# Forward and gradients of two attention and two gated MLP layers: more transposes made by DMA, weight loads moved, a saved tensor laid out by pairs of tiles

## The chip, the cores and the metric

The kernel runs on one core of one Trainium2 chip, as one launch. The metric is the device time in microseconds, given as the median of the runs shown. A profiled execution is one run of its own; the trace and the profile come from it. The engines are TensorE (PE: matmuls and transposes; PEld: its weight loads), VectorE (DVE), ScalarE (ACT), GpSimd (POOL) and SyncE (SP). SP issues all the DMAs of this kernel; a "queue of SP" is the order in which it does so, and an issue that has to wait for a semaphore holds up all issues behind it. A DMA with `transpose=True` transposes blocks on its way.

## The reference

Everything is bf16; S = 2048 rows, D = 512, F = 1376, 32 heads of 16. The input passes through four residual layers, A, B, A, B, and both A layers use the same weights, as do both B layers:

```
def _A_ref(x, wqkv, wo):                 # linear attention, phi(t) = t+1 if t > 0 else exp(t)
    q, k, v = heads of (x @ wqkv)
    pq, pk = phi(q), phi(k)
    kv = einsum("bhsd,bhse->bhde", pk, v);  z = sum of pk over s
    o = (pq . kv) / (pq . z + 1e-6)
    return o @ wo
def _B_ref(x, w_gate, w_up, w_down):
    return (sigmoid(x @ w_gate) * (x @ w_up)) @ w_down
x = A_x
x = x + _A_ref(_layernorm(x), A_wqkv, A_wo);  x = x + _B_ref(_layernorm(x), B_w_gate, B_w_up, B_w_down)
x = x + _A_ref(_layernorm(x), A_wqkv, A_wo);  x = x + _B_ref(_layernorm(x), B_w_gate, B_w_up, B_w_down)
```

The outputs are x and, for a given gradient of it, the gradients of A_x, A_wqkv, A_wo, B_w_gate, B_w_up and B_w_down (a gradient of a weight is the sum over its two layers).

## The kernel before

**Tiles and stages.** The rows are cut into 16 tiles of 128 (`st` 0 to 15); x stays in SBUF in f32. The four layers have the numbers 0 to 3. The program runs through these stages, with the times of the profiled execution: `kq_fwd` of layer 0 (keys and queries, 0 to 64 us); `ab_fwd`, which ends the attention of layer 0 and computes the MLP of layer 1 ("layer 1" below, 64 to 216 us); `kq_fwd` of layer 2 (to 290 us); `ab_fwd` for layers 2 and 3 ("layer 3", to 408 us); then backward `b_bwd_p1` of layer 3 (to 545 us), `a_bwd_p1` of layer 2 (phase 1 to 610 us, a short chain of products, phase 2 to 685 us), a stretch of weight gradients alone (to 747 us), `b_bwd_p1` of layer 1 (to 885 us), `a_bwd_p1` of layer 0 (phase 1 to 953 us, phase 2 to 1030 us), and the rest of the weight gradients (the "tail", to the end).

**Order of the work.** The order on TensorE, VectorE, ScalarE and GpSimd is the order in which the program is written (`manual_schedule`). The order of SP's queue is made by a scheduler from the order of the program and from what each DMA depends on; `issue_after(x)` pins a DMA behind the instruction x.

**`ab_fwd`, one tile.** The products g and u (L906) in three slices of 512, 512 and 352 columns; ScalarE's sigmoids (L908); VectorE's hh = u * sigmoid(g) (L911); GpSimd's second factor (L912); the attention output of a later tile (L868); then hh is transposed and multiplied by w_down one tile later (`finish`, L935). hh is transposed in one of two ways: on TensorE, in 4+4+3 blocks, with ScalarE copying them out of PSUM (L920, L923), or by one DMA (`dma_T`, L928), for which GpSimd first clears the padding of the tile. `HH_DMA` (L816) says which tiles go by DMA: 10 to 14 in layer 1, 2 to 14 in layer 3. In tiles that go by DMA, the copies of the transposed layer norm (hT) go to ScalarE instead of VectorE. At the end of a tile its saved tensors are stored (`ssd`, `hdd` and `hdl`; the last is the last piece of hh), and `side[st]` is called: in layer 1 it runs one of 13 **weight units** of `wT_units`, each of which loads up to 512 columns of a weight transposed by DMA (`wt_st`), its store to DRAM following with the next unit (wdT, wuT, wgT, woT and wqkvT: the backward pass reads them from there); in layer 3 it is a load of a backward weight, at tiles 2, 5 and 8.

**Backward attention, `a_bwd_p1`.** At its start `load_a_weights` (L251) loads woT, wqkvT and MT. Phase 1, per tile: the product dp (L1549) of MT and the transposed gradient of the tile; a chain on VectorE that ends in dq, which overwrites `phq_ld`; every second tile `dqk_store` (L1464) stores the dq of two tiles. The gradient is transposed on TensorE for tiles 0 to 7 (`gT`), and for tiles 8 to 11 and 12 to 15 by one DMA each from `g_all` (`gTb`, L1504), issued at tiles 4 and 8 (`GTLOAD`). Then GT (L1577). Phase 2, per tile: `T2_ps` (L1702), the transposes of dq and, for tiles 0 to 3, of pk, on TensorE, with ScalarE's copy to `pdT`; the product dpk (L1707); VectorE's dk, transposed on TensorE (L372); and `finish` (L1674), 12 matmuls of the transposed dq, pk and dk with weights. Inputs are loaded by pairs of tiles: `pk_ld`, `dq_ld` (two loads), `hT_ld`, `h_ld` (L1100, L1608) and, from tile 4 on, `pkT` transposed by DMA (L1599) behind hT.

**Weight gradients, `P2`.** These are products over all 16 tiles, cut into jobs of up to 256 columns. A job reads a set of saved columns (`p2_set`, L1298; three buffers, loaded up to two jobs ahead) and multiplies it with h (`p_a`; L1440) or with the gradient (L1424). ScalarE copies the result of layers 3 and 2 to an output stage `dw_stg`, which is stored to DRAM (L1397); for layers 1 and 0 VectorE adds that part to the result (L1414) and the sum goes to the output. The stage has two buffers. `W.run(n)` runs n pieces of jobs; phase 1 slips one behind each tile. In the tail they run without other work, and between them `a_small_grads` (L1760) loads saved matrices transposed and computes the rest of the gradients of A, with outputs in `fin_o`, a tile that comes from the same pool as the stage.

**The saved dq and dk.** `sv_dqk` (L111) has the dimensions [group of 256 columns, partition, tile, column]: `dqk_store` writes 512 bytes per row and group, and a set load reads 8 KB per partition in one run.

Of the kernel before, what the change touches and what calls it, by code (L numbers as in the profile page):

```python
# [18 lines left out]
D = 512  # L19
# [41 lines left out]
def kernel(  # L61
# [42 lines left out]
    for l in range(4):  # L104
        d = {}
        d["h"] = dram.tile([S, D], BF16, name=f"sv_h{l}")
        d["gbf"] = dram.tile([S, D], BF16, name=f"sv_gbf{l}")
        if l % 2 == 0:
            for nm in ("hT", "pqn", "phq", "pk"):
                d[nm] = dram.tile([S, D], BF16, name=f"sv_{nm}{l}")  # L110
            d["dqk"] = dram.tile([2 * D // GW, P, NST, GW], BF16, name=f"sv_dqk{l}")  # L111
            d["X"] = dram.tile([D, D], BF16, name=f"sv_X{l}")
            d["G"] = dram.tile([D, D], BF16, name=f"sv_G{l}")
            for nm, w in SMALL:
                d[nm] = dram.tile([P, NDC, w], BF16, name=f"sv_{nm}{l}")
            d["MT"] = dram.tile([D, D], BF16, name=f"sv_MT{l}")
        else:
            d["ssd"] = dram.tile([S, 2, F], BF16, name=f"sv_ssd{l}")
            d["hdd"] = dram.tile([3, NG, P, NST, GW], BF16, name=f"sv_hdd{l}")
            d["hdl"] = dram.tile([3, P, NST, F - NG * GW], BF16, name=f"sv_hdl{l}")  # L120
        k.sv[l] = d
    k.wT = dict(
        wqkvT=dram.tile([3 * D, D], BF16, name="wqkvT_d"),
        woT=dram.tile([D, D], BF16, name="woT_d"),
# [16 lines left out]
    with tc.tile_pool(name="wfwd", bufs=1, reuse_waits="tile") as wfwd, ExitStack() as lctx, tc.manual_schedule(engines=EM):  # L141
# [44 lines left out]
        with tc.tile_pool(name="aq0", bufs=1, reuse_waits="tile") as aq:  # L186
            A = kq_fwd(k, aq, 0, lns[0], lns[1], x_bf)
            with tc.tile_pool(name="wt_stage", bufs=2, reuse_waits="tile") as wt_stage:
                units = wT_units(k, wt_stage, A_wqkv, A_wo, B_w_gate, B_w_up, B_w_down)
                A.tail()  # L190
                ab_fwd(k, A, lns[1], {st + 1: u for st, u in enumerate(units)}, nxt=lns[2])
# [54 lines left out]
    if True:  # L246
        def load_b_weights():
            for ld in b_weight_loads():
                ld()

        def load_a_weights(l):  # L251
            woT_GT = wb.tile([P, 2, NDC, D], BF16, name="woT_GT", tag="w_b")
            k.woT, k.GT = woT_GT[:, 0, :, :], woT_GT[:, 1, :, :]
            nc.sync.dma_start(out=k.woT, in_=k.wT["woT"].rearrange("(c p) j -> p c j", p=P))
            k.wqkvT = wb.tile([P, 3 * NDC, D], BF16, name="wqkvT", tag="w_a")
            nc.sync.dma_start(out=k.wqkvT[:], in_=k.wT["wqkvT"].rearrange("(c p) j -> p c j", p=P))
# [66 lines left out]
        with tc.manual_schedule(engines=EM):  # L323
# [3 lines left out]
            sg = a_small_grads(k, tail, R.stage)  # L327
# [66 lines left out]
def wT_units(k, stage, A_wqkv, A_wo, B_w_gate, B_w_up, B_w_down):  # L394
# [33 lines left out]
    for src, nm, C in ((A_wo, "woT", D), (A_wqkv, "wqkvT", 3 * D)):  # L428
        for c0 in range(0, C // P, NDC):
            units.append(by_rows(src, c0, NDC, k.wT[nm]))  # L430

    def step():
        old = stores[:]
        stores.clear()
        if units:
            units.pop(0)()
        for store in old:
            store()
    return [step] * (len(units) + 1)
# [376 lines left out]
HH_DMA = {1: range(10, NST - 1), 3: range(2, NST - 1)}  # L816
# [70 lines left out]
def ab_fwd(k, A, ln, side, nxt=None, out_cb=None, last_cb=None):  # L887
# [3 lines left out]
    with ExitStack() as ctx:  # L891
# [61 lines left out]
        for st in range(NST):  # L953
# [3 lines left out]
                     hh=wide.tile([P, FP], BF16, name="hh_t"),  # L957
# [66 lines left out]
            nc.sync.dma_start(out=sv["hdl"][0, :, st, :], in_=T["hh"][:, NG * GW:F])  # L1024
            if st in side:
                side[st]()
# [269 lines left out]
def p2_set(k, R, src):  # L1296
    t = R.sets.tile([P, NST, R.set_w], BF16, name="p2_set")
    R.eng().dma_start(out=t[:, :, 0:src.shape[-1]], in_=src)  # L1298
# [25 lines left out]
def a_jobs(k, l):  # L1324
    return [("wqkv", k.sv[l]["dqk"][g, :, :, :], g * GW, GW) for g in range(2 * D // GW)]
# [7 lines left out]
class P2:  # L1333
# [67 lines left out]
    def units(self):  # L1401
        k, R, nc = self.k, self.R, self.k.nc
        i = 0
        while True:
# [5 lines left out]
            ov = p2_stage_tile(R, "b")  # L1410
# [50 lines left out]
def dqk_store(k, sv, half, b, nb, src):  # L1461
    n = D // GW
    for g in range(n):
        k.nc.sync.dma_start(out=sv["dqk"][half * n + g, :, b * nb:(b + 1) * nb, :],  # L1464
                            in_=src[:, :, g * GW:(g + 1) * GW])


def a_bwd_p1(k, R, l, W, mk_out_cb=None):
# [6 lines left out]
    with ExitStack() as ctx:  # L1475
# [9 lines left out]
        with tc.tile_pool(name=f"ab_stg1{l}", bufs=3, side="right", reuse_waits="tile") as stg, \  # L1485
# [38 lines left out]
            def dq_ops(T):  # L1524
# [9 lines left out]
                if st % NB2 == NB2 - 1:  # L1534
                    dqk_store(k, sv, 0, st // NB2, NB2, T["ph_pair"][:])
# [7 lines left out]
            for st in range(NST):  # L1543
                ph_st = phld.get(st)
                T = dict(st=st, ph=ph_st, ph_pair=phld.cur)
# [40 lines left out]
        with tc.tile_pool(name=f"ab_stg2{l}", bufs=2, side="right", reuse_waits="tile") as stg, \  # L1586
# [14 lines left out]
            def load(p):  # L1601
# [5 lines left out]
                for g in range(D // GW):  # L1607
                    nc.sync.dma_start(out=dq[:, :, g * GW:(g + 1) * GW], in_=sv["dqk"][g, :, st0:st0 + NB2, :])  # L1608
                hTld.get(st0)
                LD[p] = dict(pk=pkld.cur, dq=dq, hT=hTld.cur)  # L1610
                if st0 >= NB:
                    with tc.issue_after(hTld.ins.ins):
                        load_pkT(p)
# [76 lines left out]
            for st in range(NST):  # L1690
                L = LD[st // NB2]
                e = st % NB2
                pk_st, dq_st, hT_st = L["pk"][:, e, :], L["dq"][:, e, :], L["hT"][:, e, :]
# [4 lines left out]
                pdT = work.tile([P, 2, NDC, P], BF16, name="pdT")  # L1698
                tps = ps_tile(k, "t", [P, 2, NDC, P], BF16, "T2_ps")
                for a, src in enumerate((dq_st, pk_st)[0:1 + own]):  # L1700
                    for c in range(NDC):
                        nc.tensor.transpose(tps[:, a, c, :], src[:, c * P:(c + 1) * P], k.ident[:])  # L1702
                nc.scalar.copy(pdT[:, 0:1 + own, :, :], tps[:, 0:1 + own, :, :])
                T["dqT"] = pdT[:, 0, :, :]
                T["pkT"] = pdT[:, 1, :, :] if own else pkT[st // NB2][:, :, e * P:(e + 1) * P]
# [7 lines left out]
                if e == NB2 - 1:  # L1713
                    dqk_store(k, sv, 1, st // NB2, NB2, dkst[:])
# [45 lines left out]
def a_small_grads(k, pool, stg):  # L1760
# [13 lines left out]
    for c in range(NDC):  # L1774
# [3 lines left out]
        o = stg.tile([P, D], BF16, name="fin_o")  # L1778
# [3 lines left out]
    for ic in range(NDC):  # L1782
# [5 lines left out]
        o = stg.tile([P, D], BF16, name="fin_o")  # L1788
# [33 lines left out]
```

## Time and profile before

| what | value |
| --- | --- |
| runs before | 1160.11, 1161.38, 1163.07 us; median 1161.38 us |
| profiled execution | 1164.9 us, of which the span of the trace is 1163.2 us |
| TensorE clock, mean granted | 0.999 of full speed |
| busy, share of the span | PE 97%, DVE 60%, ACT 46%, POOL 25% |
| DMA | 281.33 MB in 365220 packets, 242 GB/s on average |
| SP's data queue | 82.0% of 16 DMA engines' span |

The span is the time between the first and the last instruction of the trace; the device time has 1.7 us around it. A busy share is the time in which an engine has at least one instruction under way. The DMA share is the time that packets took, as a part of what 16 DMA engines have; the trace has it above 1 in some short windows. In lines of the timeline, the first number is the start and the second the duration in microseconds, followed by engine, source line, operation, output and inputs, shape and count; a bracket tells how long the engine was idle before, and what released it. A line of windows gives the window, its length, the busy time and number of instructions of PE, PEld, DVE, ACT and POOL, then the granted clock, the DMA share and GB/s.

### The profile page before, as it was taken

The numbers are of one execution on the slowest core, as the hardware profiler recorded it, in microseconds if no ns is written. First come the engines' busy times: TensorE is split into PE (matmuls) and PEld (weight loads), VectorE is DVE, ScalarE is ACT, GpSimd is POOL, SyncE is SP. The second block draws the span as 40 slices with busy tenths as digits, with TensorE's granted clock in tenths as the row PEclk, the third lists the DMA queues.
The fourth block names the chain that finished last, engine by engine and source line by source line (L and its number), as shares of the span: only waits on it lengthen the run. The fifth ranks groups of instructions, "written<-read, shape, count | busy, mean of one in ns | idle before, by whom it ended". The sixth has DMA issues, their size and how long they took to land.

```text
span 1163.2 us, 20084 instructions
## 1 busy us (share of the span) xinstructions
PE 1127.2 (97%) x7414; PEld 672.2 (58%) x7524; DVE 698.3 (60%) x1343; ACT 529.8 (46%) x983; POOL 287.7 (25%) x514
## 2 busy tenths in 40 slices
PE   8979999998999999999999999999999999999988
PEld 4445444444455555555456578855557755548878
DVE  6778876667767456664975740166664976741211
ACT  6667666546665644444625531244344516510001
POOL 5646667435666400000110120000000111210000
PEclk9999999999999999999999999999999999999999
DMA  8969997858677899997889979468977788859985
GB/s 267 304 185 267 286 267 218 253 157 282 202 209 229 252 273 284 312 278 223 221 243 273 283 207 344 119 191 245 275 248 235 192 280 246 224 185 298 262 185 167
DMA packets 365220, 281.33 MB, mean 242 GB/s; under 512 B 141184, under 2 KB 350016, under 8 KB 360256
## 3 DMA queue, kind: packets, MB, share of 16 engines
q1 hardware_dynamic: 365120, 280.03, 82.0%
q8 instruction: 59, 0.97, 0.3%
q14 instruction: 41, 0.34, 0.1%
HBM read 136.71 MB, written 117.80 MB: 219 GB/s over the span
## 4 chain that ended last, share of the span: by engine, by line
PE 87%; DVE 6%; DMA 4%; ACT 2%; issue 1%; POOL 0%; DVEq 0%; ACTq 0%; SPq 0%; POOLq 0%
PE p_ps L1440 17%; PE dh_ps L1200 13%; PE dh_ps L1674 7%; PE p_ps L1424 7%; PE dhh_ps L1077 6%; PE u_ps L906 5%; PE g_ps L906 5%; PE y_ps L935 5%; PE T_ps L1160 3%; PE GT_ps L1577 2%; PE dp_ps L1549 2%; PE dpk_ps L1707 2%; PE y_ps L868 2%; PE t_mm L613 2%; PE X_ps L621 2%
## 5 line engine op out<-in xcount | busy, mean ns | idle before, releaser
L1440 PE MATMUL p_ps<-p_set,p_a 128*128 128x256 bf16 (+1 forms) x2032 | 211.4, 265 | 3.4 <-DVE dw_stg L1414 3.3
L1440 PEld LDWEIGHTS <-p_a 128*128 128x128 bf16 x2048 | 186.2, 98 | 26.7 <-DMA p_set<-sv_dqk 2.3
L1085 DVE TENSOR_TENSOR dd<-dhh_ps,ssd 128x512 bf16<-128x512 f32 x144 | 82.5, 629 | 129.9 <-PE dhh_ps L1077 128.9
L1164 ACT COPY ddT<-T_ps 128x1024 bf16<-128x1024 bf16 (+1 forms) x96 | 83.0, 867 | 132.1 <-PE T_ps L1160 131.7
L912 POOL TENSOR_TENSOR ssd_t<-hh_t,oms 128x512 bf16<-128x512 bf16 (+1 forms) x96 | 101.5, 1064 | 47.7 <-ACT hT L381 24.7
L1200 PEld LDWEIGHTS <-ddT 128*128 128x128 bf16 (+1 forms) x704 | 68.7, 98 | 72.2
L1051 POOL TENSOR_SCALAR ab<-c 128x2 f32<-128x2 f32 x64 | 12.3, 192 | 393.1 <-DVE junk L1048 378.9
L906 PEld LDWEIGHTS <-hT 128*128 128x128 bf16 x768 | 72.2, 98 | 63.8 <-DVE hT L379 1.4
L911 DVE TENSOR_TENSOR hh_t<-u_ps,ssd_t 128x512 bf16<-128x512 f32 (+1 forms) x96 | 60.5, 634 | 61.7 <-PE u_ps L906 42.8
L1414 DVE TENSOR_TENSOR dw_stg<-p_ps,dw_stg 128x512 bf16<-128x512 f32 (+3 forms) x43 | 28.0, 654 | 109.0 <-PE p_ps L1440 82.5
L906 PE MATMUL u_ps<-wu,hT 128*128 128x512 bf16 (+1 forms) x379 | 89.6, 357 | 0.5
L906 PE MATMUL g_ps<-wg,hT 128*128 128x512 bf16 (+1 forms) x366 | 86.5, 356 | 1.7 <-DVE hT L379 1.0
L1200 PE MATMUL dh_ps<-wgT,ddT 128*128 128x512 bf16 (+1 forms) x344 | 84.8, 379 | 0.3
L908 ACT ACTIVATE ssd_t<-g_ps 128x512 bf16<-128x512 f32 (+1 forms) x96 | 53.3, 555 | 66.4 <-PE g_ps L906 58.3
L935 PE MATMUL y_ps<-wd,hhT 128*128 128x512 bf16 (+1 forms) x346 | 80.5, 379 | 0.9 <-DVE x L937 0.6
L1200 PE MATMUL dh_ps<-wuT,ddT 128*128 128x512 bf16 (+1 forms) x340 | 80.7, 379 | 0.6
L1424 PE MATMUL p_ps<-p_a,p_set 128*128 128x512 bf16 (+1 forms) x344 | 80.4, 379 | 0.4
L1043 ACT ACTIVATE t_sb<-dh_ps,rstd_all 128x512 f32<-128x512 f32 x64 | 44.0, 687 | 77.5 <-issue 41.8
L1077 PE MATMUL dhh_ps<-wdT,gTb 128*128 128x512 bf16 (+1 forms) x328 | 73.3, 357 | 0.4
L1048 DVE SCALAR_TENSOR_TENSOR junk<-t_sb,h_ld 128x512 bf16<-128x512 f32 x64 | 44.0, 688 | 42.9 <-ACT t_sb L1043 42.1
L935 PEld LDWEIGHTS <-hhT 128*128 128x128 bf16 (+1 forms) x352 | 33.9, 98 | 39.3 <-issue 0.7
L1424 PEld LDWEIGHTS <-p_set 128*128 128x128 bf16 (+1 forms) x352 | 33.5, 100 | 34.9
(225 smaller groups left out, 1914.5 us busy)
## 6 DMA issues: line engine op xcount, KB each, us to landing
p_set<-sv_hdd SPq DMA_DIRECT2D x30, 1024.0 KB, 7.3
sv_ssd<-ssd_t SPq DMA_DIRECT2D x32, 688.0 KB, 4.4
ssd<-sv_ssd SPq DMA_DIRECT2D x24, 688.0 KB, 5.4
sv_hdd<-dd SPq DMA_DIRECT2D x48, 320.0 KB, 3.9
sv_hdd<-hh_t SPq DMA_DIRECT2D x32, 320.0 KB, 4.6
h_ld<-sv_h SPq DMA_DIRECT2D x32, 256.0 KB, 4.9
p_a<-sv_h SPq DMA_DIRECT2D x16, 512.0 KB, 6.3
p_set<-sv_dqk SPq DMA_DIRECT2D x8, 1024.0 KB, 7.0
```

What stands on the lines that cost most here:

```text
L906: nc.tensor.matmul(ps[:, 0:w], lhsT=hT[:, kc, :], rhs=w_sb[:, kc, c0:c0 + w], start=(kc == 0), stop=(kc == NDC - 1))
L908: nc.scalar.activation(ssd_t[:, 0, c0:c0 + w], g_ps[:, 0:w], ACT.Sigmoid)
L911: nc.vector.tensor_tensor(hh_t[:, c0:c0 + w], u_ps[:, 0:w], ssd_t[:, 0, c0:c0 + w], ALU.mult)
L912: nc.gpsimd.tensor_tensor(ssd_t[:, 1, c0:c0 + w], hh_t[:, c0:c0 + w], oms[:, 0:w], ALU.mult)
L935: nc.tensor.matmul(y_ps[:], lhsT=T["hhT"][0:r, fc, :], rhs=k.wd[0:r, fc, :], start=(fc == 0), stop=(fc == NFC - 1))
L1077: k.nc.tensor.matmul(ps[:, 0:w], lhsT=gT[:, jc, :], rhs=k.wdT[:, jc, c0:c0 + w], start=(jc == 0), stop=(jc == NDC - 1))
L1085: k.nc.vector.tensor_tensor(dd[:, a, c0:c0 + w], ps[:, 0:w], ssd[:, a, c0:c0 + w], ALU.mult)
L1164: nc.scalar.copy(ddT[:, :, f0:f0 + nfull, :], tps[:, :, 0:nfull, :])
L1200: nc.tensor.matmul(T["dh"][:], lhsT=ddT_block(T, a, fc), rhs=(k.wuT, k.wgT)[a][0:r, fc, :], start=(i == 0), stop=(i == 2 * NFC - 1))
L1424: nc.tensor.matmul(ps[0:r, :], lhsT=set_t[:, st, c * P:c * P + r], rhs=self.ops[j["l"], "g"][:, st, :], start=(st == 0), stop=(st == NST - 1))
L1440: nc.tensor.matmul(ps[:, icl * w:(icl + 1) * w], lhsT=self.ops[j["l"], "h"][:, st, ic * P:(ic + 1) * P], rhs=set_t[:, st, 0:w], start=(st ...
L1674: nc.tensor.matmul(dh_ps[:], lhsT=lhsT, rhs=rhs, start=(i == 0), stop=(i == len(ops) - 1))
```

## The change

It has seven parts.

1. `HH_DMA` of layer 1 becomes tiles 2 to 14, and the tile `hh_t` has three buffers there.
2. `wT_units` keeps only the nine units of the B weights. They run as `piece`: two before the first tile of layer 1, the others at tiles 0, 2, ..., 12, and `flush` does the last stores at tile 14. Work at the end of a tile, in layer 3 too, is now pinned behind the store of `hdl` of that tile.
3. woT and wqkvT are no longer prepared. `load_a_weights` keeps four DMAs back that load A_wo and the three blocks of A_wqkv (v, q, k) transposed; `a_bwd_p1` issues one at each of tiles 4, 6, 8 and 10 of phase 1, pinned behind the load of `phq`.
4. `sv_dqk` becomes [group, pair of tiles, partition, tile of the pair, column]. A store by `dqk_store` keeps its runs of 512 bytes per row but covers one stretch of DRAM; a set load reads eight runs of 1 KB per partition.
5. In phase 2, dq of the tiles 4 to 15 is loaded transposed, by two DMAs per pair behind the load of hT, and `pkT` behind them. The transposes of dq on TensorE and the copy to `pdT` stay for tiles 0 to 3 only. As rows of two tiles alternate in the saved layout, `finish` takes every second column of the loaded block as its weights.
6. `load_b_weights` holds the load of w_gate transposed back: behind the load of hT of pair 6 of the attention backward before it.
7. The stage `dw_stg` of the jobs ("b") has three buffers, and `fin_o` has three buffers in a pool of its own.

In all, TensorE loses 184 transposes (88 in layer 1, 96 in phase 2), ScalarE 48 instructions and VectorE 8; GpSimd gets 8 more. In the program built from it, SP's queue has the transposes of wqkv of tiles 6 and 8 between the two loads of `gTb` of phase 1.

```
-            d["dqk"] = dram.tile([2 * D // GW, P, NST, GW], BF16, name=f"sv_dqk{l}")
+            d["dqk"] = dram.tile([2 * D // GW, NST // 2, P, 2, GW], BF16, name=f"sv_dqk{l}")
...
-                units = wT_units(k, wt_stage, A_wqkv, A_wo, B_w_gate, B_w_up, B_w_down)
+                piece, flush = wT_units(k, wt_stage, B_w_gate, B_w_up, B_w_down)
+                piece()
+                piece()
                 A.tail()
-                ab_fwd(k, A, lns[1], {st + 1: u for st, u in enumerate(units)}, nxt=lns[2])
+                ab_fwd(k, A, lns[1], {**{st: piece for st in range(0, 14, 2)}, NST - 2: flush}, nxt=lns[2])
...
         def load_b_weights():
-            for ld in b_weight_loads():
-                ld()
+            wd, wu, wg = b_weight_loads()
+            wd()
+            wu()
+            with tc.issue_after(k.hold):
+                wg()
...
-            nc.sync.dma_start(out=k.woT, in_=k.wT["woT"].rearrange("(c p) j -> p c j", p=P))
             k.wqkvT = wb.tile([P, 3 * NDC, D], BF16, name="wqkvT", tag="w_a")
-            nc.sync.dma_start(out=k.wqkvT[:], in_=k.wT["wqkvT"].rearrange("(c p) j -> p c j", p=P))
+            lds = [(k.woT, A_wo[:, :])]
+            lds += [(k.wqkvT[:, c:c + NDC, :], A_wqkv[:, c * P:(c + NDC) * P]) for c in (2 * NDC, 0, NDC)]
+            k.a_weight_loads = [lambda o=o, i=i: nc.sync.dma_start(out=o, in_=i, transpose=True) for o, i in lds]
...
-HH_DMA = {1: range(10, NST - 1), 3: range(2, NST - 1)}
+HH_DMA = {1: range(2, NST - 1), 3: range(2, NST - 1)}
...
-                     hh=wide.tile([P, FP], BF16, name="hh_t"),
+                     hh=wide.tile([P, FP], BF16, name="hh_t", bufs=3 if l == 1 else 2),
...
-            nc.sync.dma_start(out=sv["hdl"][0, :, st, :], in_=T["hh"][:, NG * GW:F])
+            ins = nc.sync.dma_start(out=sv["hdl"][0, :, st, :], in_=T["hh"][:, NG * GW:F])
             if st in side:
-                side[st]()
+                with tc.issue_after(ins.ins):
+                    side[st]()
...
-            ov = p2_stage_tile(R, "b")
+            ov = p2_stage_tile(R, "b", 3)
...
                 ph_st = phld.get(st)
+                if st % 2 == 0 and 4 <= st < 12:
+                    with tc.issue_after(phld.ins.ins):
+                        k.a_weight_loads.pop(0)()
...
-                for g in range(D // GW):
-                    nc.sync.dma_start(out=dq[:, :, g * GW:(g + 1) * GW], in_=sv["dqk"][g, :, st0:st0 + NB2, :])
+                if st0 < NB:
+                    for g in range(D // GW):
+                        nc.sync.dma_start(out=dq[:, :, g * GW:(g + 1) * GW], in_=sv["dqk"][g, p])
                 hTld.get(st0)
+                if st0 >= NB:
+                    dq = dq[:].rearrange("p n d -> p (n d)").rearrange("p (c t) -> p c t", c=NDC)
+                    with tc.issue_after(hTld.ins.ins):
+                        n = GW // P
+                        for g in range(D // GW):
+                            nc.sync.dma_start(out=dq[:, g * n:(g + 1) * n, :],
+                                              in_=sv["dqk"][g, p].rearrange("p n w -> (p n) w"), transpose=True)
+                        load_pkT(p)
                 LD[p] = dict(pk=pkld.cur, dq=dq, hT=hTld.cur)
-                if st0 >= NB:
-                    with tc.issue_after(hTld.ins.ins):
-                        load_pkT(p)
+                if p == 6:
+                    k.hold = hTld.ins.ins
...
-                pdT = work.tile([P, 2, NDC, P], BF16, name="pdT")
-                tps = ps_tile(k, "t", [P, 2, NDC, P], BF16, "T2_ps")
-                for a, src in enumerate((dq_st, pk_st)[0:1 + own]):
-                    for c in range(NDC):
-                        nc.tensor.transpose(tps[:, a, c, :], src[:, c * P:(c + 1) * P], k.ident[:])
-                nc.scalar.copy(pdT[:, 0:1 + own, :, :], tps[:, 0:1 + own, :, :])
-                T["dqT"] = pdT[:, 0, :, :]
-                T["pkT"] = pdT[:, 1, :, :] if own else pkT[st // NB2][:, :, e * P:(e + 1) * P]
+                if own:
+                    pdT = work.tile([P, 2, NDC, P], BF16, name="pdT")
+                    tps = ps_tile(k, "t", [P, 2, NDC, P], BF16, "T2_ps")
+                    for a, src in enumerate((L["dq"][:, e, :], pk_st)):
+                        for c in range(NDC):
+                            nc.tensor.transpose(tps[:, a, c, :], src[:, c * P:(c + 1) * P], k.ident[:])
+                    nc.scalar.copy(pdT[:], tps[:])
+                    T["dqT"], T["pkT"] = pdT[:, 0, :, :], pdT[:, 1, :, :]
+                else:
+                    T["dqT"], T["pkT"] = L["dq"][:, :, e:NB2 * P:NB2], pkT[st // NB2][:, :, e * P:(e + 1) * P]
...
-        o = stg.tile([P, D], BF16, name="fin_o")
+        o = pool.tile([P, D], BF16, name="fin_o", bufs=3)
```

## The prediction

> **What bounds the kernel now.** I read the busy times first, then the chain of work that ended last, and after that TensorE's instructions in order of time, stage by stage.
>
> ```profile
> PE 1127.2 (97%) x7414; PEld 672.2 (58%) x7524; DVE 698.3 (60%) x1343; ACT 529.8 (46%) x983; POOL 287.7 (25%) x514
> ...
> PE 87%; DVE 6%; DMA 4%; ACT 2%; issue 1%; POOL 0%; DVEq 0%; ACTq 0%; SPq 0%; POOLq 0%
> ```
>
> TensorE is busy 97% of the span and carries 87% of the chain. In order of time, nearly all its gaps lie before 304 us and in one place near 1125 us; between them it has two, of 0.4 and 0.3 us. So an instruction taken off TensorE is worth its pitch, a transfer costs nothing until TensorE waits for it, and the question is which transfer will be late. DMA has little room: its engines are busy 82% of the span.
>
> **Transposes of hh in layer 1 (tiles 2 to 9).** Each of these tiles has 4+4+3 transposes on TensorE (L920). The start of the attention product (L868) marks a tile.
>
> ```profile
> 90.66 1.02 PE L868 MATMUL y_ps<-M_sb,pqnT 128*128 128x512 bf16 x4
> ...
> 106.97 0.33 PE L920 MATMUL t_tp<-ident,hh_t 128*128 128x128 bf16 x3
> ...
> 180.81 1.03 PE L868 MATMUL y_ps<-M_sb,pqnT 128*128 128x512 bf16 x4
> ...
> 291.19 1.03 PE L868 MATMUL y_ps<-M_sb,pqnT 128*128 128x512 bf16 x4
> ...
> 372.82 1.03 PE L868 MATMUL y_ps<-M_sb,pqnT 128*128 128x512 bf16 x4
> ```
>
> The first and third lines are tiles 2 and 12 of layer 1: 90.15 us. The last two are tiles 2 and 12 of layer 3, the same loop with tiles 2 to 14 already transposed by DMA: 81.63 us. The changed layer 1 has layer 3's TensorE order, so the gain is **8.5 us** if the transfers keep up. Of it, 8 x 11 x 0.056 = 4.9 us are the transposes (four start 0.22 us apart in a row); the rest are waits around them. The eight tiles' ACT copies go too. POOL gets eight small memsets and ACT takes over eight hT copies from DVE; both are busy under 80% there.
>
> Do the transfers keep up? DMA's share is the last but one column here, by stretch:
>
> ```profile
> 90.66:165.85 75.19, 72.55 (x457) 38.08 (x464) 60.79 (x112) 53.19 (x105) 50.16 (x81) 1.00 0.96 277
> ...
> 641.80:649.60 7.80, 7.75 (x50) 4.01 (x49) 6.02 (x12) 4.41 (x11) 1.62 (x4) 1.00 1.18 302
> ```
>
> A 256-byte packet takes 25 ns on average in the trace's packet records, one of 1 KB 50 ns. An hh transpose is 1408 packets of 256 bytes, 2.2 us of 16 engines; a weight unit is 2048 such packets and 512 of 1 KB, 4.8 us. Four of thirteen units go (19 us) and eight transposes come (18 us): the load stays, in a stage 8.5 us shorter. Tiles already transposed by DMA show 5.6 to 6.2 us of DMA each (0.67 to 0.75 of 8.3); with a unit every second tile that is 8.0 to 8.6 us per tile of 8.33. So DMA runs at its limit. A tile transpose is issued at 173.10 and used at 181.67: 8.6 us, against 3.6 us to landing (median of 18, longest 5.1). The third hh buffer removes DVE's two waits for the hdl store (4.1 us). Bounds: 0 and 11 tiles at 8.8 us, 5 us; I take a **loss of 1 us**, since the slack is over twice what a unit adds.
>
> The Trainium skill (VectorE: DVE Perf Modes, "The three transpose paths" and its rules) speaks against this: 390 ns for a 128x128 transpose on TensorE, 1309 ns by DMA, and TensorE preferred where PSUM will do. By it eleven blocks would be an estimated 14.4 us, past the 8.6. The trace disagrees: 3.6 us for eleven, and 56 ns of TensorE's time each.
>
> **Query gradients transposed by DMA.** Phase 2 of the attention backward, any tile from 4 on:
>
> ```profile
> 982.12 0.39 PE L372 MATMUL t_ps<-ident,dkstage 128*128 128x128 bf16 x4
> 982.35 0.39 PE L1702 MATMUL T_ps<-ident,dq_ld 128*128 128x128 bf16 x4
> 982.57 0.81 PE L1707 MATMUL dpk_ps<-Nv,hT_ld 128*128 128x512 bf16 x3
> ...
> 986.02 0.39 PE L372 MATMUL t_ps<-ident,dkstage 128*128 128x128 bf16 x4
> ```
>
> Removing L1702's four transposes leaves 3.90 - 0.22 = 3.68 us per tile: 0.224 x 12 tiles x 2 layers = **5.4 us**. What is late next? DVE has 3.25 us per tile (0.75+0.74+0.69+0.69+0.29+0.08), under 3.68; ACT loses the 0.60 us pdT copy. The strided weights cost nothing: L1200's come with stride 2 and load in 98 ns like all others. A pair's two transposes replace two loads: 1024 packets of 256 bytes for 512 of 512 (28 ns), 0.7 us more DMA per pair, and about 1 us more on SP's queue. Their buffer now comes free only with the dh product, so they are issued behind the two transfers' waits as pkT is today; from there to use is some 8 us, against 4.2 us for pkT (3.0 to 6.1). In layer 2 DMA is at 1.04 to 1.18 for three pairs and TensorE does not wait; the gate weights (1.4 MB) leave that stretch, and their first use is over 80 us behind their new place. Bounds 0 and -4 (one tile per layer lost); I take **-0.5 us**.
>
> **Weights transposed in the backward pass.** This is the step that moves SP's queue. In the order built, SP has the transposes of wqkv between those of g_all. Layer 2 now:
>
> ```profile
> 574.33 3.03 SPq L1504 DMA_TRANSPOSE gTb<-g_all  x1
> 577.41 1.08 SPq L1464 DMA_DIRECT2D sv_dqk<-phq_ld  x2
> 578.59 0.45 SPq L1397 DMA_DIRECT2D dwp_wd<-dw_stg  x1
> 579.08 0.59 SPq L1298 DMA_DIRECT2D p_set<-sv_hdl  x1
> ```
>
> ```profile
> 582.74 1.03 PE L1549 MATMUL dp_ps<-MT,gTb 128*128 128x512 bf16 x4
> ```
>
> ```profile
> DMA to landing us min/median/max: 4.4/5.3/6.2
> ```
>
> The first line is the second gTb (tiles 12 to 15), landed at 578.7, used by the product at 582.74. After, the three lines below it and two wqkv transposes stand ahead of it. An issue of such a transpose takes 2.6 us (median of wt_st from wqkv). First gTb ends 569.9; dqk 1.2, wqkv 2.6, phq 0.4, p_set 0.6, dqk 1.1, dwp 0.5, wqkv 2.6: issue at 579, landing 5.3 later, **2 us late** (0 to 5). Layer 0: first gTb ends 912.4; dqk 1.05, wqkv 2.6, phq 0.4, wqkv 2.6, a wait for the job's end at 920.0, dwp, dqk, p_set: issue at 922, landing 927 to 929, used at 927.4: **1 us late** (0 to 5). Behind them on SP wait query loads and dqk stores; DVE, which runs some 3 us behind TensorE by tile 8 or 9, takes that up (0 to -3 in layer 0, counted in the range). The first transpose of g_all keeps its place and its 0.3 us gap. wo and wqkv land some 20 us ahead of use.
>
> **Moved loads and the new layout.** Layer 3's three backward weight loads (4 us of DMA each) leave the stage before, where nothing waited for them, for tiles 2, 5 and 8, at share 0.77 (0 to -2; I take -0.3). The dqk stores keep their packets; a set load becomes 1024 packets of 1 KB (50 ns) for 128 of 8 KB (368 ns): 3.2 for 2.9 us, hidden except in the tail.
>
> **Tail.**
>
> ```profile
> 1127.12 0.10 PEld L1440 LDWEIGHTS <-p_a 128*128 128x128 bf16 x1 [2.29 <-DMA p_set<-sv_dqk]
> ...
> 1128.21 0.62 DVE L1414 TENSOR_TENSOR dw_stg<-p_ps,dw_stg 128x192 bf16<-128x192 f32 x2 [6.51 <-DMA out_dram<-dw_stg]
> ...
> 1128.62 4.91 PE L1440 MATMUL p_ps<-p_set,p_a 128*128 128x256 bf16 x32 [3.30 <-DVE dw_stg L1414]
> ```
>
> ```profile
> 1128.60:1131.20 2.60, 2.58 (x13) 1.79 (x13) 0.24 (x1) 0.58 (x1) 0.00 (x0) 0.50 0.81 209
> ```
>
> TensorE stops 3.3 us: first for the dqk set, then for DVE, which waits for an output store to free one of two dw_stg buffers. The third buffer ends that 1.4 us. The granted clock after the stop is 0.50, and those 32 matmuls take 4.91 instead of 3.66 us: 1.25 us more. The set now lands 0.3 to 0.5 later. A stop of 2.1 us at 71 us left the clock at 1.00, so I let the shorter stop here keep it. Gain 1.4 + 1.25 - 0.45 = **2.2 us**; from 1 (clock falls all the same) to 4.9 (no stop).
>
> By the Trainium skill (TensorE: Matmul & The Clock Gate, "What's actually happening") an idle window of about 3.4 us halves the clock; this row, 0.50 after 3.3 us, agrees. By it the shorter stop keeps the clock too; so the sum is the same.
>
> **Sum**, against the profiled execution (span 1163.2, time 1164.9): 8.5 - 1 + 5.4 - 0.5 - 3 - 0.3 + 2.2 = 11.3 us less, 1153.6. The median shown is 1161.4, 3.5 below that execution, so the forecast is **1150.1**.
>
> **Rivals.** (1) Every cover holds: 8.5 + 5.4 + 4.9 = 18.8, 1142.6. For it, 4 us of slack before the second gTb and none lost in layer 3; against it, SP's order. (2) The gTb waits grow to 5 us in each layer and halve the clock each time (1.3 us): 12.6 lost instead of 3, gain 1.7, 1159.7. For it, SP's transposes reach 4.1 us. (3) The change doesn't do what it says: layer 1 stays at its 9.4 us per tile because DMA, not the transposes, paces it; then 7.5 go, 1157.6. For it, the share of 0.96; against it, much of that was thirteen units at one per tile. (4) Slower: hh transposes in layer 1 land later than 8.6 us after issue, and each tile waits for its own. It decides from 10 us on (8 tiles x 1.4 us eat the 11.3); at 10.6 us, 16 us, 1166. For it, transposes at a share of 1.03 in the tail land in 7.1 us (median, up to 8.2); against it, 5.1 is the longest for this one.
>
> **Chances.** Forecast 0.52 (its own range 1146 to 1155), rival 1 0.14, rival 2 0.14, rival 3 0.11, rival 4 0.09. Leaving out rival 4 and part of rivals 1 and 2, the range is 1143.5 to 1159. A measurement of this kernel can tell about 0.3% from no change, that is under 1157.9 for faster: 0.52 + 0.14 + 0.05 + 0.07 = 0.78; same 0.13; slower 0.09.
>
> **What would show it.** Tile 2 to tile 12 of layer 1 in 82 to 84 us (over 88 is rival 3, a wait on hhT is rival 4); 3.68 us per tile in phase 2 with no wait on dq_ld or pkT; a wait of TensorE on gTb of about 2 and 1 us; a stop under 3 us near the end, at full clock. Most wrong would I be if SP's queue, not DMA, set the pace somewhere that I did not add up.

## The result, and the profile after

The changed kernel takes **1157.3 us** (median of 6 runs, 1155.16 to 1159.55), against 1160.95 us before (6 runs, 1159.59 to 1163.31). The ratio is 0.9958, with a 95% interval from 0.9943 to 0.9974. By the ratio that is some 4.9 us less, by the two medians 3.7, where 11.3 were forecast. The sign was right and the time lies in the range, but the gain is less than half of the forecast one. The profiled execution took 1157.5 us, its span is 1155.8.

The busy times and the chain of the profile after:

```profile
PE 1124.4 (97%) x7340; PEld 663.5 (57%) x7340; DVE 692.4 (60%) x1335; ACT 509.2 (44%) x935; POOL 289.9 (25%) x522
...
PE 86%; DVE 8%; DMA 3%; ACT 2%; issue 1%; SPq 1%; POOL 0%; DVEq 0%; ACTq 0%
```

TensorE still bounds the kernel. Before, nearly all of its gaps were in the forward pass, apart from the stop near 1125 us; now two stand in the backward pass, at 574.5 and 922.6 us, with two smaller ones near 671 and 674. (I give the length of a stop by TensorE's weight loads. A bracket on a matmul is up to 0.5 us shorter, as the last matmul ends later than the last weight load.) To see what each part did, I cut the span by the starts of TensorE's instructions, matmuls and weight loads: the first transpose of g_all opens phase 1 of a layer, the first load of woT_GT ends it, phase 2 goes from the first transpose of pk to the last dkT, and the tail is what follows. (The two short chains of products between the phases, 8.7 us each, are the same in all. The expectations below cut phase 2 and the tail some tenths differently.)

| stage, us | before | before, second profile | after | after, second profile |
| --- | --- | --- | --- | --- |
| to phase 1 of layer 2 | 547.13 | 547.69 | 539.23 | 539.48 |
| phase 1, layer 2 | 62.12 | 62.12 | 65.99 | 64.87 |
| phase 2, layer 2 | 66.63 | 67.04 | 66.16 | 64.44 |
| between | 207.05 | 207.05 | 207.06 | 207.06 |
| phase 1, layer 0 | 62.24 | 62.24 | 66.69 | 67.39 |
| phase 2, layer 0 | 66.59 | 66.59 | 63.91 | 63.91 |
| tail | 134.08 | 130.55 | 129.38 | 129.48 |
| span | 1163.21 | 1160.65 | 1155.80 | 1154.00 |

The second profiles come from the experiments. The first row and the rows of phase 2, where the change takes transposes off TensorE, got shorter, and so did the tail; the rows of phase 1, where nothing was taken off, got 2.7 to 5.2 us longer.

**Layer 1 gained all of its 8.5 us.** Tiles 2 and 12, and the window between them:

```profile
90.81 1.03 PE L873 MATMUL y_ps<-M_sb,pqnT 128*128 128x512 bf16 x4
172.45 1.03 PE L873 MATMUL y_ps<-M_sb,pqnT 128*128 128x512 bf16 x4
```

```profile
90.81:172.45 81.64, 81.15 (x460) 41.44 (x459) 64.19 (x127) 53.66 (x99) 62.98 (x108) 1.00 0.94 258
```

It takes 81.64 us where it took 90.15, with TensorE busy for 81.15 of them and a DMA share of 0.94. No tile waits for its hhT.

Layer 3 gave a part back. One tile there, which TensorE enters at 331.0 us, takes 8.90 us instead of 8.33, and 9.74 in the second profile. It comes after the load of wuT, one of the three weight loads that the change pins behind the store of hdl: the hhT that SP issues next takes 4.32 us to issue, the stores behind it go out late, and VectorE waits for an hdl store to free an hh buffer:

```profile
333.65 0.69 DVE L916 TENSOR_TENSOR hh_t<-u_ps,ssd_t 128x512 bf16<-128x512 f32 x1 [3.80 <-DMA sv_hdl<-hh_t]
```

Every profile of a kernel with the whole change, with or without the moves below, has this tile 0.6 to 1.5 us longer; none of the profiles without it has. No run was made to take the change in layer 3 out alone.

**The second gTb is late.** SP's queue in phase 1 of layer 2, between the two loads:

```profile
557.55 2.98 SPq L1512 DMA_TRANSPOSE gTb<-g_all  x1
560.64 1.49 SPq L1473 DMA_DIRECT2D sv_dqk<-phq_ld  x2
562.19 2.53 SPq L260 DMA_TRANSPOSE wqkvT<-in_A_wqkv_dram  x1
...
569.22 2.35 SPq L260 DMA_TRANSPOSE wqkvT<-in_A_wqkv_dram  x1
571.62 3.24 SPq L1512 DMA_TRANSPOSE gTb<-g_all  x1
```

and what TensorE does at that time:

```profile
573.12 1.89 PE L1433 MATMUL p_ps<-p_a,p_set 128*128 128x512 bf16 x8
577.01 1.04 PE L1560 MATMUL dp_ps<-MT,gTb 128*128 128x512 bf16 x4 [2.01 <-DMA gTb<-g_all]
577.89 0.24 PE L1528 MATMUL dz_ps<-cneg_bf,pqn_all 128*128 128x8 bf16 x4
577.99 3.42 PE L1433 MATMUL p_ps<-p_a,p_set 128*128 128x512 bf16 x8
```

The load is issued at 571.62 and lands some 5.3 us later. TensorE started its last matmul ahead of it at 574.62; its weight loads stand still from 574.51 to 577.01, a stop of 2.50 us. The last line shows a second cost: eight matmuls that took 1.89 us ahead of the stop take 3.42 behind it. The granted clock (last column but two) tells why:

```profile
574.50:577.00 2.50, 0.50 (x3) 0.01 (x1) 2.46 (x6) 0.00 (x0) 0.52 (x1) 1.00 0.95 227
577.00:578.00 1.00, 0.99 (x9) 0.52 (x10) 0.90 (x3) 0.00 (x0) 0.00 (x0) 1.00 0.65 155
579.00:580.00 1.00, 1.00 (x4) 0.37 (x3) 0.62 (x2) 0.00 (x0) 0.00 (x0) 0.50 1.22 261
580.00:581.00 1.00, 1.00 (x4) 0.36 (x3) 0.97 (x4) 0.00 (x0) 0.00 (x0) 0.50 1.87 305
582.00:584.00 2.00, 2.00 (x14) 0.98 (x13) 1.97 (x5) 0.61 (x2) 0.52 (x1) 1.00 1.00 348
```

The clock falls only after TensorE has begun again, and is at half for some 3.4 us (the windows from 578 to 582 have means of 0.59, 0.50, 0.50 and 0.70). So a stop of 2.50 us made the stage 3.87 us longer. In layer 0 the stop is 3.13 us and the stage 4.45 us longer; the issue of the load alone takes 5.33 us there:

```profile
916.98 5.33 SPq L1512 DMA_TRANSPOSE gTb<-g_all  x1
925.71 1.30 PE L1560 MATMUL dp_ps<-MT,gTb 128*128 128x512 bf16 x4 [2.64 <-DMA gTb<-g_all]
```

**The dq transposes** gave their 2.68 us in layer 0, but in layer 2 the last pair was late:

```profile
670.30 1.03 PE L1728 MATMUL dpk_ps<-Nv,hT_ld 128*128 128x512 bf16 x4
672.89 1.06 PE L1693 MATMUL dh_ps<-wqkvT,dq_ld 128*128 128x512 bf16 x4 [1.56 <-DMA dq_ld<-sv_dqk]
```

**The tail** has no stop any more. The 32 matmuls that took 4.91 us at half clock:

```profile
1122.44 3.66 PE L1449 MATMUL p_ps<-p_set,p_a 128*128 128x256 bf16 x32
```

It seems to give 4.7 us, of which the experiments leave little.

### The profile page after: what moved, and what is told of

Read it like the earlier page. It is cut to its first block, busy times and chain, and to the rows that moved or that the text cites. A ratio compares the mean times of both kernels' runs of the same rounds, so it can differ in the third digit from the quotient of the medians.

```text
span 1155.8 us, 19770 instructions
## 1 busy us (share of the span) xinstructions
PE 1124.4 (97%) x7340; PEld 663.5 (57%) x7340; DVE 692.4 (60%) x1335; ACT 509.2 (44%) x935; POOL 289.9 (25%) x522
## 4 chain that ended last, share of the span: by engine, by line
PE 86%; DVE 8%; DMA 3%; ACT 2%; issue 1%; SPq 1%; POOL 0%; DVEq 0%; ACTq 0%
PE p_ps L1449 16%; PE dh_ps L1206 13%; PE dh_ps L1693 7%; PE dhh_ps L1083 6%; PE y_ps L940 6%; PE u_ps L911 6%; PE g_ps L911 6%; PE p_ps L1433 5%; PE T_ps L1166 3%; PE t_mm L618 2%; PE GT_ps L1588 2%; PE dpk_ps L1728 2%; PE y_ps L873 2%; PE X_ps L626 2%; DMA gTb<-g_all 1%; PE t_ps L376 1%
## 5 line engine op out<-in xcount | busy, mean ns | idle before, releaser
L911 PE MATMUL g_ps<-wg,hT 128*128 128x512 bf16 (+1 forms) x384 | 90.0, 357 | 1.0 <-DVE hT L383 1.0
L1433 PE MATMUL p_ps<-p_a,p_set 128*128 128x512 bf16 (+1 forms) x352 | 84.1, 389 | 0.0
L1083 PE MATMUL dhh_ps<-wdT,gTb 128*128 128x512 bf16 x336 | 74.2, 357 | 0.0
L1054 DVE SCALAR_TENSOR_TENSOR junk<-t_sb,h_ld 128x512 bf16<-128x512 f32 x64 | 46.8, 731 | 37.2 <-ACT t_sb L1049 28.7
```

The costliest lines, as they stand in the source:

```text
L911: nc.tensor.matmul(ps[:, 0:w], lhsT=hT[:, kc, :], rhs=w_sb[:, kc, c0:c0 + w], start=(kc == 0), stop=(kc == NDC - 1))
L1083: k.nc.tensor.matmul(ps[:, 0:w], lhsT=gT[:, jc, :], rhs=k.wdT[:, jc, c0:c0 + w], start=(jc == 0), stop=(jc == NDC - 1))
L1433: nc.tensor.matmul(ps[0:r, :], lhsT=set_t[:, st, c * P:c * P + r], rhs=self.ops[j["l"], "g"][:, st, :], start=(st == 0), stop=(st == NST - 1))
```

## The experiments

My theory after the traces: SP's order makes the second gTb late, the gate weights make the last dq late, and the two buffers of the output stage make the stop in the tail of before. The rivals are named with each run. All ratios are to the kernel before, with the 95% interval.

**The weight loads behind the second gTb.**

```
-                if st % 2 == 0 and 4 <= st < 12:
+                for _ in range({10: 1, 12: 1, 14: 2}.get(st, 0)):
                     with tc.issue_after(phld.ins.ins):
                         k.a_weight_loads.pop(0)()
```

> The changed kernel, with the four transposed loads of A_wo and A_wqkv moved from tiles 4, 6, 8, 10 of phase 1 to tiles 10, 12, 14, 14, so that SP issues all four behind the second load of gTb; they are the same DMAs and stay in phase 1. Theory: SP's order made the second gTb late. Then TensorE's gaps of 2.50 us (at 574.5) and 3.13 us (at 922.6) go, the clock stays at 1.00 there, phase 1 of layer 2 falls from 65.99 to about 62.1 us and of layer 0 from 66.70 to about 62.2, and the kernel is 8.3 us faster than the changed one, near 1149. Rival: the transposed loads fill the DMA engines and gTb lands late wherever they stand in phase 1. Then it gains under 3 us, and the transfers of gTb take longer than the 4.4 to 6.2 us of before.

Measured: 1152.89 us, ratio 0.9915 (0.9898 to 0.9933), against 0.9958 for the change. SP's queue in layer 2 is now

```profile
557.69 3.02 SPq L1512 DMA_TRANSPOSE gTb<-g_all  x1
560.82 1.24 SPq L1473 DMA_DIRECT2D sv_dqk<-phq_ld  x2
562.51 0.38 SPq L1408 DMA_DIRECT2D dw_stg<-dwp_wd  x1
563.77 0.37 SPq L1106 DMA_DIRECT2D phq_ld<-sv_phq  x1
564.18 3.02 SPq L1512 DMA_TRANSPOSE gTb<-g_all  x1
```

The second gTb is issued 6.5 us behind the first, not 14.1, and both loads land 4.4 to 5.1 us after their issue in both layers. TensorE's two stops are gone; phase 1 takes 62.12 us in layer 2 and 63.52 in layer 0, where a new wait of 1.21 us stands at its end. The same transposes, in the same stage, stop TensorE nowhere in layer 2 when they stand behind gTb, and for 1.2 us in layer 0: the order on SP was the cause, and the rival falls. The other profiles say the same: the four with transposes of A_wqkv between the two loads (the change twice, and the kernels with the gate weights moved and with two hh buffers) all have both stops, of 2.2 to 3.9 us, and the three with them behind have neither. The profiled execution, at 1149.0 us, was the fastest of six; by the ratios the kernel gains 5 us on the change and not 8.3. The other five runs lie 3.1 to 4.5 us above the profiled one, and what they lose stays open.

**The gate weights behind the last pair.** `k.hold` is the load of pkT, of which the last is that of pair 7:

```
-                if p == 6:
-                    k.hold = hTld.ins.ins
...
-                    nc.sync.dma_start(out=pkT[b][:], in_=sv["pk"][batch_rows(b, NB2), :], transpose=True)
+                    k.hold = nc.sync.dma_start(out=pkT[b][:], in_=sv["pk"][batch_rows(b, NB2), :], transpose=True).ins
```

> The changed kernel, with the load of w_gate transposed pinned behind pkT of pair 7 instead of hT of pair 6, so that no part of it stands ahead of a pair's dq transposes on SP. Theory: the two parts of w_gate ahead of pairs 6 and 7 make the dq transposes of pair 7 late. Then TensorE's gaps of 2.05 and 0.77 us near 671 to 674 go, phase 2 of layer 2 falls from 66.54 to about 64.3 us as in layer 0, and the kernel is 2.2 us faster than the changed one, near 1155. Rival: the pair's transposes are late from the load on DMA (share 1.14 in the stretch 660 to 671) whatever w_gate does. Then over 1.5 us of the gap stays, and the time within 1 us of 1157.

Measured: 1156.21 us, 0.9952 (0.9935 to 0.9970). The profile shows what was expected: phase 2 of layer 2 takes 64.33 us, 1.8 less, and the waits for dq and pkT there are gone (one of 0.69 us ahead of a transpose of dk is left). By the median the difference to the change is within the uncertainty. The second profile of the change explains it: there phase 2 took 64.44 us as well. The least that any run here shows is 63.95 us, so the loss is 0.5 us in one execution and 2.2 in the other. With the gate weights in the change's place, the four profiles have 66.16, 64.44, 66.23 (two hh buffers) and 64.06 us (weight loads behind gTb); with them moved, the three have 64.33, 63.95 and 63.95. So the move takes away a loss that comes in some executions only, and that the gate weights alone make it is not shown.

**The buffers of the output stage alone**, and the kernel before once more.

```
-            ov = p2_stage_tile(R, "b")
+            ov = p2_stage_tile(R, "b", 3)
...
-        o = stg.tile([P, D], BF16, name="fin_o")
+        o = pool.tile([P, D], BF16, name="fin_o", bufs=3)
```

> The kernel before, with the output stage of the weight gradients in three buffers and fin_o in three buffers of a pool of its own, and nothing else of the change. Theory: the stop of 2.29 and 1.41 us near 1125 and the half clock behind it come from the two buffers; then the tail (from the last product of phase 2 in layer 0 to the end) falls from 133.98 to 129.3 us, and the kernel is 4 to 5 us faster than before, near 1156.5. Rival: the profiled execution of before, 4 us above the median of its runs, was the odd one, and most executions have no such stop; then the time is within 1 us of 1161 and only the profile's tail is shorter.

> The kernel before once more, for a second profile. Theory: its tail again shows TensorE stopped for some 3.5 us near 1125 us, with the granted clock at 0.50 behind it, and takes about 134 us. Rival: the stop was that execution's own; then the tail takes 129 to 131 us, and the span is near 1159.2.

Measured: 1161.43 us with the buffers, ratio 0.9990 (0.9980 to 1.0001). The kernel before, again, took 1162.36 us, close to the median of the 18 runs beside it, 1161.85, and its tail is 130.55 us:

```profile
1125.69 0.59 PE L1777 MATMUL sg_ps<-GT_ld,kvbd_ld 128*128 128x512 bf16 x2
1127.32 3.65 PE L1440 MATMUL p_ps<-p_set,p_a 128*128 128x256 bf16 x32 [1.04 <-DVE dw_stg L1414]
```

The same place, with one stop of 1.3 us in place of 2.29 and 1.41, and the 32 matmuls at full clock: 3.65 us, not 4.91. So the profile that I predicted from had a tail that the second one does not have. The buffers do take the stop away (129.43 us of tail), and are worth about 1 us by the profiles and the ratio, whose interval still reaches to no gain, and 0.4 by the medians. The theories of both runs fall, and both rivals were right about the tail.

**hh alone.** The kernel before with only `HH_DMA` of layer 1 as tiles 2 to 14 and three buffers for `hh_t`; all 13 units stay.

> The kernel before, with only the hh of tiles 2 to 9 of layer 1 transposed by DMA (and three hh buffers); all 13 weight units stay, one at each of tiles 1 to 13. Theory: a tile needs 5.6 to 6.2 us of DMA and a unit 4.8, which is 10.4 to 11.0 per tile against 8.33 of TensorE, so DMA sets the pace: layer 1 from tile 2 to tile 12 takes 88 to 100 us and the kernel is not faster than before (a ratio of 0.998 to 1.01); the change gained its 8.5 us there because four units left the stage and the others stand at every second tile. Rival: transfers were never the limit, the stage takes about 82 us with 13 units as well, and the kernel is 8.5 us faster (0.993).

Measured: 1166.69 us, ratio 1.0030 (1.0016 to 1.0043): slower. Tiles 2 to 12 of layer 1:

```profile
89.77:183.36 93.59, 83.32 (x460) 40.73 (x459) 63.45 (x127) 54.32 (x99) 61.77 (x108) 1.00 1.06 270
```

93.59 us with TensorE busy for 83.32 and a DMA share of 1.06. Removing 88 transposes from TensorE alone makes this stage 3.4 us longer. Transfers set the pace: from 100 to 190 us ScalarE waits 26.9 us for stores of ssd to free its buffers, VectorE waits 26.2 us for ScalarE, and TensorE 5.1 us for VectorE's hh and 2.3 us for hhT. In the change four units left this stage, and the other nine stand at every second tile, behind the store of hdl. Together that turned the loss into 8.5 us of gain; the runs do not separate the two. The theory holds.

**dq alone.** The kernel before with the layout and the transposed loads of dq; the gate weights load where they did.

> The kernel before, with only the new layout of dq and dk and the transposed load of dq for tiles 4 to 15; the weights of the next stage are loaded where they were. Theory: the transposes taken from TensorE are worth 2.7 us in each phase 2, and what the change lost in layer 2 came from the load of w_gate that it had placed among the pairs. Then phase 2 of layer 0 falls from 66.6 to 64.0 us and of layer 2 from 67.0 to about 64.4, and the kernel is 4.5 to 5.4 us faster (a ratio of 0.9955). Rival: the gate weights in their old place load the DMA engines in the first pairs of layer 2, where the pairs' transposes are then late; phase 2 of layer 2 stays above 66 and the gain is 2.7 us (0.9977) or less.

Measured: 1162.11 us, 0.9996 (0.9985 to 1.0006). Phase 2 of layer 0 takes 63.91 us, the expected 2.7 less; that of layer 2 takes 69.85, some 3 more:

```profile
644.94 1.15 PE L1719 MATMUL dpk_ps<-Nv,hT_ld 128*128 128x512 bf16 x4 [4.03 <-DMA hT_ld<-sv_hT]
645.88 1.91 PE L1684 MATMUL dh_ps<-wqkvT,dq_ld 128*128 128x512 bf16 x4
```

A 4 us wait for a load of hT, issued at 638.36 and landed 6.5 us later at a DMA share of 1.25, with a part of the gate weights issued 4.5 us ahead of it; and half clock behind the wait (1.91 us for four matmuls, for 1.03). My theory for this run (the pairs are in time with the gate weights in their old place) falls, and the rival, DMA full in the first pairs, is right in what it forecast. The run with hh alone, which keeps the gate weights and the transposes of dq in their old place, has waits of 1.50 and 0.42 us (by the matmuls) at the same pair, so this place is tight without the new transposes too. With the gate weights in their old place this part of the change is worth nothing.

**The change once more, both moves, and a spread version.** "Both" joins the first two edits. "Spread" leaves A_wo at tile 4, has A_wqkv at tiles 10, 12 and 14, and pins the gate weights behind the last set load of the stretch of weight gradients:

```
-                if st % 2 == 0 and 4 <= st < 12:
+                if st in (4, 10, 12, 14):
...
-    R.eng().dma_start(out=out, in_=src)
+    k.hold = R.eng().dma_start(out=out, in_=src).ins
```

> The changed kernel once more, for a second profile and for times on the same chip as the two kernels below. Theory: both waits for the second gTb are part of nearly every execution (2 to 3.9 us each) and the half clock behind them of most, so phase 1 again takes 64 to 66 us in layer 2 and 66 to 68 us in layer 0; the ratio to before is 0.995 to 0.997. Rival: the profiled execution shown first was the odd one; then one of the two waits is missing.

> The changed kernel with both moves: the four loads of A_wo and A_wqkv behind the second gTb load (tiles 10, 12, 14, 14), and w_gate transposed behind pkT of the last pair. Theory: the two losses add, so both phase 1 stay at 62.1 to 63.5 us and both phase 2 at about 64.2 us; 2 us less than with the weight loads moved alone, a ratio to before near 0.990 (the ratio of the weight move alone was 0.9915, of the gate move alone 0.9952, of the change 0.9958). Rival: the runs of the kernel with the weight loads moved, whose profiled execution lay 4 us under their median, lose those 4 us in the wait for pkT and dq that the gate load causes; then this one's median falls to 1149, a ratio near 0.988.

> The changed kernel with A_wo loaded at tile 4 as in the change and the three blocks of A_wqkv at tiles 10, 12 and 14 (all three behind the second gTb), and w_gate transposed pinned behind the last set load of the stretch of weight gradients, some 50 us later than in the change and some 20 us ahead of its first use. Theory: it keeps what the kernel with both moves gained, and loses neither its waits for sets near 700 and 715 us (1.16 and 0.46 us) nor, with one load less behind the second gTb, its 1.1 us at the end of phase 1 in layer 0; 1.5 to 2.7 us less, a ratio near 0.988. Rival: the late w_gate pushes the first transposed gradients or sets of the next stage, and TensorE waits near its start (750 us) instead; then the ratio stays at 0.989 to 0.991.

| kernel | median, us | ratio, interval | phase 1, layers 2 and 0 | phase 2, layers 2 and 0 | span |
| --- | --- | --- | --- | --- | --- |
| change again | 1156.15 | 0.9951 (0.9939 to 0.9962) | 64.87, 67.39 | 64.44, 63.91 | 1154.0 |
| both moves | 1150.08 | 0.9894 (0.9873 to 0.9915) | 62.12, 63.41 | 63.95, 63.91 | 1148.3 |
| spread | 1151.17 | 0.9902 (0.9886 to 0.9918) | 62.12, 63.17 | 63.95, 64.18 | 1146.5 |

Both stops for gTb come again in the second profile of the change, 3.07 and 3.55 us, as the theory had it. "Both moves" beats the change (0.9894 against 0.9951 and 0.9958) and takes 1150.08 us. That this is where the forecast had put the change is a coincidence: the forecast counted 3 us lost for gTb, which this kernel does not lose. Its profile has new waits of 1.16 and 0.46 us for sets at 700 and 715 us, behind the gate weights; "spread" has none of these, and no wait near 750 either. Its profiled execution is 1.8 us shorter, but by its median it is not better, so its expected 1.5 to 2.7 us did not show; the ratio is where its rival had put it, without the wait that the rival named. For "both moves" the theory's 0.990 and its rival's 0.988 both lie in the interval. Five of six runs of "both" lie between 1149.05 and 1150.39, those of "spread" between 1148.20 and 1155.07; what the runs of 1152 us and more lose was not profiled and stays open.

**Two hh buffers** in the changed kernel (the three of layer 1 back to two).

> The changed kernel with two instead of three buffers for hh in layer 1. Theory, from the prediction: the third buffer took VectorE's waits for the store of hdl away, and with two of them VectorE waits some 2 us per tile again, of which TensorE sees a part: tile 2 to tile 12 of layer 1 takes 83 to 90 us instead of 81.6, and the kernel is 1.5 us or more slower than the change. Rival: in the layer 3 loop two buffers are enough (81.63 us there), so they are here, and nothing changes.

Measured: 1158.17 us, 0.9972 (0.9961 to 0.9983), which is 0.2% above the change on the same chip. But the profile shows tiles 2 to 12 of layer 1 in 81.64 us, as with three, and one wait of VectorE for the hdl store, 1.9 us. Neither view fits the whole: the profiled execution has no loss in layer 1, the runs have some 2 us. Inconclusive.

## Why the prediction was right in sign and wrong in size

Step by step, against the second profile of before, whose time is the typical one:

| term | forecast, us | measured, first and second profile of the change |
| --- | --- | --- |
| hh in layer 1, DMA at its limit, layer 3's loads | +8.5 - 1 - 0.3 | +8.5, +8.2 |
| dq on TensorE, less what is late | +5.4 - 0.5 | +3.6, +5.3 |
| second gTb late | -3 | -8.3, -7.9 |
| tail | +2.2 | +1.2, +1.1 |
| sum | +11.3 | +4.9, +6.7 |

- **hh in layer 1: right.** The gain came out as the difference of the two layers' loops, and the estimate that four units fewer just leave room for eight transposes is borne out from the other side, by the run that kept the units. Two of the smaller terms were off and nearly cancel: DMA at its limit cost nothing of the 1 us, and layer 3's loads cost 0.6 and 1.4 us instead of 0.3. The +8.5 and +8.2 of the table are also helped by the second profile of before, in which the granted clock was at 0.50 from 61.4 to 64.8 us, just ahead of layer 1; against the first profile the row is +7.9 and +7.7, for a forecast of +7.2.
- **gTb: the mechanism right, the size wrong, and this is the step that failed.** The forecast was 2 us in layer 2 and 1 in layer 0. SP's place for the load was forecast well: 579 in the times of before is 571.1 after the 7.9 us won by then, and it was issued at 571.62. In layer 2 the wait itself was right too (2.01 us by the matmuls, 2.57 in the second profile). Two things were missed. In layer 0 I gave the transfer 5.3 us from issue to landing, its time in a quiet queue; behind two transposed weight loads and a set, issue alone took 5.33 us and landing 8.7 (in the second profile 6.36 and 8.5), against 3.0 and 5.0 when it stood ahead of them. And the sum has no price for the clock behind these stops, as I let stops under 3 us keep it, from one stop of 2.1 us that did; three of the four stops here halved it, for 1.3 to 1.6 us each. Rival 2 had both, at 12.6 us lost; the truth is between.
- **The tail, and the way to the median: wrong.** I took 2.2 us for a stop and a half clock that only the profiled execution had to that extent, and then subtracted the whole 3.5 us by which that execution lies above the median as if it were spread over everything. The first profile's tail is 3.53 us longer than the second's, so a part of the same microseconds was counted twice. The tail is worth 0.4 to 1.2 us.
- **dq: right in layer 0 to a tenth, short in layer 2** by 2.2 and 0.5 us against the 63.95 us that other runs reach. I put that down to the gate weights, of which a part is issued just ahead of the transposes of pairs 6 and 7, but it is not shown for them alone: with the same place for the gate weights, the run with the weight loads behind gTb loses 0.1. I had written that they leave that stretch; they leave its start for its end.
- **Rival 1** (all covers hold, 18.8 us) needed the second gTb in time; the run with both moves gives 12 us of it. **Rivals 3 and 4** did not happen: tile 2 to 12 takes 81.64 us, and hhT lands 4.4 us after issue (median, up to 5.4). The run with hh alone shows what rival 3 meant: with all thirteen units a tile takes 9.36 us.

## What to carry to other kernels

When transposes move from TensorE to DMA, read the queue that issues them in the built order, and ask of each load behind the new ones how long before its use it is issued; give it the transfer time of a full queue, not of a quiet one. Price a stop of TensorE with the clock that may follow it. And before summing against one profiled execution that lies above the median, look for the stage in which it does: a gain there may belong to that execution alone.

## What the runs showed of the hardware

- **A stop's length does not decide alone whether the clock falls.** In the backward pass, stops of 2.2, 2.4 and 3.07 us left it at 1.00; stops of 2.50, 3.13, 3.15, 3.55, 3.85 and 4.2 us were followed by 0.50 (as were the two of 2.29 and 1.41 us in the tail of the first profile), beginning up to 1.2 us after TensorE had resumed, for some 3.4 us. The Trainium skill (TensorE: Matmul & The Clock Gate, "What's actually happening") gives a window of about 3.4 us that runs free, so that the same stop can fall differently into it; these runs agree with that, and show that a stop well under 3.4 us can be enough.

- **How much work a stop leaves in a fixed stretch of 3.41 us separates the cases here.** In the clock records of the twelve traces each full half-clock stretch lasts 3.413 us, and within a trace the starts lie whole multiples of that apart (578.18 and 926.34 us in the profile after: 102 of them). I cut each trace on that grid and counted each matmul with the time from start to start that it takes in a run without gaps (0.216 us for 512 columns, 0.109 for 256, 0.056 for 128). Leaving the first and last microseconds of the traces out, there are some 4000 such windows. All nine with at most 35% of work were followed by half clock, of the nine between 38% and 39.1% two were, and none above that. The stop of 2.50 us in the profile after fell into one window and left 35% there. The stop of 3.07 us at the same place in the second profile fell across two and left 54% and 66%. Four of the falls, at 61 and at 252 to 260 us, stand behind no single stop over 0.8 us. This was worked out from the records; no run was made to test it.

The first two lines are the profile after (the window of the stop, and the next), the last three the second profile of the change:

```profile
574.77:578.18 3.41, 1.40 (x11) 0.61 (x10) 3.27 (x8) 0.05 (x1) 0.52 (x1) 1.00 0.92 220
578.18:581.59 3.41, 3.41 (x9) 1.18 (x8) 2.56 (x6) 0.69 (x2) 0.52 (x1) 0.50 1.16 238
573.11:576.52 3.41, 2.14 (x14) 0.81 (x12) 3.27 (x8) 0.66 (x2) 0.52 (x1) 1.00 1.31 168
576.52:579.93 3.41, 2.10 (x14) 1.04 (x15) 2.27 (x5) 0.59 (x1) 0.52 (x1) 1.00 0.97 254
579.93:583.34 3.41, 3.41 (x21) 1.61 (x20) 3.11 (x7) 1.17 (x2) 0.48 (x1) 1.00 1.08 234
```

- **The issue of a transposed load can hold SP for long.** One of A_wqkv took 2.0 to 2.6 us in the change and up to 7.12 us in the kernel with both moves, some 4 us behind the load of h for the weight gradients (2 MB); the load of phq issued just ahead of it landed 8 us after its issue, and VectorE waited 5.1 us for it:

```profile
925.65 7.12 SPq L260 DMA_TRANSPOSE wqkvT<-in_A_wqkv_dram  x1
933.17 0.69 DVE L1537 SCALAR_TENSOR_TENSOR phq_ld<-phq_ld,rden_all 128x512 bf16<-128x512 bf16 x1 [5.07 <-DMA phq_ld<-sv_phq]
```
